# Eleven kept chunks instead of twelve, and whole V chunks beside the serial chain, in a two-layer cached-attention decode kernel

## The chip, the core and the metric

The kernel runs on one core of a Trainium2 chip. The metric is the device time of one execution in microseconds (us), and the runs' median stands for the kernel. The profile is one further execution, taken by the hardware profiler; its span (first to last instruction of the program) is a little shorter than its device time.

Engines are called as in the profile: PE is the matmul engine (PEld its weight loads), DVE the vector engine, ACT the scalar engine, POOL GpSimd, SP the queue that issues the loads.

## What is computed

One new token for each of 8 sequences goes through attention (A), an MLP mixer (B), A again and B again, with the same weights and the same K and V caches in both rounds:

```python
x = x + _A_ref(_layernorm(x, axis=-1), A_k_cache, A_v_cache, A_wq, A_wo)
x = x + _B_ref(_layernorm(x, axis=-1), B_w1, B_w2, B_w3, B_w4)
x = x + _A_ref(_layernorm(x, axis=-1), A_k_cache, A_v_cache, A_wq, A_wo)
x = x + _B_ref(_layernorm(x, axis=-1), B_w1, B_w2, B_w3, B_w4)
```

Attention has 16 query heads on 8 KV heads, 4096 cached positions, head width 256, model width 448. In B the shifted branch vanishes (the sequence length is 1), so that what is left is x + h2 with the gelu MLP of width 1792. The K and V caches together are 8 x 8 x 4096 x 256 x 2 tensors of bf16, 268 MB, and each of the two rounds needs all of them.

## The kernel before

**Chunks and places.** The caches come in chunks of 1 MB (128 partitions of 4096 bf16 elements). A unit is one (round, sequence b, KV head pair gp), with four K chunks and four V chunks. On chip there are `NC = 15` places of one chunk each (the tile `places`). A list `places` of free ones is filled in the program's order: a chunk's place goes back on it when its item has been recorded, and `emit_loads` then hands it to the next load. All cache loads are issued by SP in this one order; a load waits on SP until the instructions that still read its place are done.

**Kept chunks.** Round 2 of a sequence needs the same K and V as round 1. For two head pairs (gp 3 and gp 2) a list `kept` names chunks which stay in their places between round 1 and round 2 of the sequence: 8 K chunks (already transposed) and 4 V chunks. One more V chunk (`inner`) waits in PSUM (`away`, `back`; lines 791 to 803) and a quarter of another (`part`). So, when all 12 kept chunks of a sequence are on chip, 15 - 12 = 3 places are left for the stream of other chunks.

**Work on a chunk.** A K chunk is transposed in place by DVE (`transpose_k`, line 759, three instructions), two transposed chunks are scored by 32 matmuls of 256 columns (`scores`, line 774; 64 of 128 columns where the two places are not neighbours), then ACT takes exponentials (line 783). A V chunk takes 16 matmuls (`pv`, line 827) into a PSUM bank `o`.

**The chain.** When round 1 of sequence b is done, a serial chain of small steps makes the queries of its round 2: `half` (normalise the attention output, lines 451 to 479), `add_cols` with wo (line 365), `norm` (lines 226 to 306, with a power on POOL at line 254), the MLP (lines 383 and 365), `norm` again, and `project_q` (line 316, four blocks of 32 matmuls). It is a Python generator; each `yield` ends a step, and `step(idx)` records the next step of the generators of the kinds "chain", "last" and "rest". The kept K chunks can be scored for round 2 only when the chain has ended.

**What stands beside the chain.** `first_kept` puts off the V chunks of up to four units of other sequences (16 chunks; for the last two chains only two units, 8 chunks). `AFTER = 8` of them are placed right after round 1 of the sequence, beside the chain, and the rest between the kept K chunks of round 2. The first `AFTER + 3` of them are in the set `narrow`: each of these is loaded by two DMAs of half a chunk (line 749), and around its `pv` four steps are recorded: one before, two after its first 8 matmuls, one after it. So a half chunk of V has two steps behind it:

```python
            step(idx)
            ...
                pv(
                    st["o", g8],
                    ...
                    (lambda: (step(idx), step(idx))) if it in narrow else None,
                )
        ...
        emit_loads()
        step(idx)
```

Generators of kind "last" (they close round 2 of an earlier sequence) are stepped in the same calls. If the first kept K is reached and the chain has not ended, `while (1, b) not in state: step(...)` records the rest of it with nothing between.

The order of work in one sequence's period, in the middle of the run, is thus: round 1 of gp 2 and gp 3 (their chunks stay), interleaved with K of two other units; 8 V chunks beside the chain; 8 kept K with 8 V between them; kept V; then gp 0 and gp 1 of round 2 and the next sequence. There are eight such periods, one for each sequence.

Of the kernel before, what the change touches and what calls it, by code (L numbers as in the profile page):

```python
# [17 lines left out]
def kernel(  # L18
# [37 lines left out]
    GP = G // 2  # L56
# [5 lines left out]
    NP = 4  # L62

    kept = [(gp, 0, n) for gp in (GP - 1, GP - 2) for n in range(4)]
    kept += [(GP - 1, 1, n) for n in range(1, 4)] + [(GP - 2, 1, 2)]
    inner = (GP - 2, 1, 1)
    part = (GP - 1, 1, 0)
    Q4 = 4 * Dh
# [141 lines left out]
    def norm(x, nb, twice):  # L210

        def room(name, shape, at):
            n = shape[0] * shape[1]
            if nb < Bn:
                t = chn.tile([128, n * MID], FP32, tag=name)
                ap = t[:, 0 : n * nb]
            else:
                ap = scratch(at, n * nb)  # L220
            return ap.rearrange("p (s f b) -> p s f b", s=shape[0], f=shape[1])

        def bc(ap):
            return ap.unsqueeze(1).to_broadcast([128, 4, nb])

        xx = room("xx", (2, 4), 0)
        nc.vector.tensor_mul(xx[:, 0], x, wv[:].unsqueeze(2).to_broadcast([128, 4, nb]))
        nc.vector.tensor_mul(xx[:, 1], xx[:, 0], x)
        xs = room("xs", (1, 2), 512)[:, 0]
        nc.vector.tensor_reduce(  # L230
            xs, xx.rearrange("p s f b -> p s b f"), mybir.AxisListType.X, ALU.add
        )
        yield
        st = room_ps("st", nb).rearrange("p (s b) -> p s b", b=nb)
        nc.tensor.matmul(st, ones, xs, start=True, stop=True)  # L235
        yield
        mv = room("mv", (1, 2), 528)[:, 0]
        nc.vector.tensor_copy(mv, st)
        var = room("var", (1, 1), 608)[:, 0, 0]
        if nb == 1:  # L240
            nc.vector.scalar_tensor_tensor(
                var, mv[:, 0], mv[:, 0], mv[:, 1], ALU.mult, ALU.subtract, reverse1=True
            )
        else:
            nc.vector.tensor_mul(var, mv[:, 0], mv[:, 0])
            nc.vector.tensor_sub(var, mv[:, 1], var)


        ve = room("ve", (1, 2), 544)[:, 0]
        n = 2 if twice else 1  # L250
        rs = room("rs", (1, 2), 560)[:, 0]

        def power(k0, k1):
            nc.gpsimd.tensor_tensor(  # L254
                rs[:, k0:k1].rearrange("p n b -> p (n b)"),
                ve[:, k0:k1].rearrange("p n b -> p (n b)"),
                nhalf[:].to_broadcast([128, (k1 - k0) * nb]),
                ALU.pow,
            )

        if twice and nb == 1:
            nc.vector.scalar_tensor_tensor(
                ve[:, :, 0], var.to_broadcast([128, 2]), 0.0, eps2[:], ALU.max, ALU.add
            )
            power(0, 2)
        else:
            if twice:
                nc.vector.tensor_scalar(
                    ve[:, 1], var, 0.0, EPS * EPS / (1 + EPS), ALU.max, ALU.add
                )  # L270
                power(1, 2)
            nc.vector.tensor_scalar(ve[:, 0], var, 0.0, EPS, ALU.max, ALU.add)
            power(0, 1)
        xc = room("xc", (1, 4), 576)[:, 0]
        nc.vector.tensor_tensor(xc, x, bc(mv[:, 0]), ALU.subtract)  # L275
        yield
        if nb > 1:
            yield
        c = (1 + EPS) ** -0.5 if twice else 1.0
        rl = rs[:, n - 1]  # L280
        parts = ((0, 128, 0, 0, 3, 0), (0, 64, 64, 3, 4, 4), (64, 128, 64, 3, 4, 3))
        if nb == 1:
            nc.vector.scalar_tensor_tensor(  # L283
                xbs(1)[:, 0:4, 0], xc[:, :, 0], rl, low[:, int(twice)], ALU.mult, ALU.mult
            )
            parts = parts[1:2]
        for p0, p1, x0, f0, f1, to in parts:
            pp = slice(x0, x0 + p1 - p0)
            dst = xbs(nb)[p0:p1, to : to + f1 - f0, :]
            if nb == 1:  # L290
                nc.vector.tensor_scalar(dst, xc[pp, f0:f1], rl[pp], c, ALU.mult, ALU.mult)
            else:
                nc.vector.scalar_tensor_tensor(
                    dst,
                    xc[pp, f0:f1],
                    c,
                    rl[pp].unsqueeze(1).to_broadcast([p1 - p0, f1 - f0, nb]),
                    ALU.mult,
                    ALU.mult,
                )  # L300
        if twice and nb == 1:
            nc.vector.scalar_tensor_tensor(x, xc, rs[:, 0], x, ALU.mult, ALU.add)
        elif twice:
            nc.vector.tensor_tensor(xc, xc, bc(rs[:, 0]), ALU.mult)
            nc.vector.tensor_add(x, x, xc)
        yield
# [174 lines left out]
    locked = []  # L481
# [68 lines left out]

    tasks, items, due = [], [], []
    number, narrow = {}, set()
    AFTER = 8

    def block(k, v=None):

# [15 lines left out]
    def first_kept(b, units, before):  # L572

        k2, k3 = ((0, b, gp) for gp in keep)
        todo = list(units)
        block(todo.pop(0), before)
        if len(todo) > 2:
            block(todo.pop(0))
        block(k2)
        block(todo.pop(0), k2) if todo else block(None, k2)  # L580
        block(k3)
        block(todo.pop(0), k3) if todo else block(None, k3)
        assert not todo
        items.extend(due)
        due.clear()
        for u in units:
            due.extend((number[u], 1, c) for c in range(4))
        narrow.update(due[: AFTER + 3])
        items.extend(due[:AFTER])
        del due[:AFTER]  # L590

# [3 lines left out]
    for b in range(Bn):  # L595
# [5 lines left out]
        else:  # L601
            block((1, b, free[0]), k2)
            block((1, b, free[1]), (1, b, free[0]))
            block(None, (1, b, free[1]))
    saved = {u for units in ahead for u in units}

    def stays(it):
        n, kv, c = it
# [10 lines left out]
    loads = [it for it in items if not (tasks[it[0]][0] == 1 and (stays(it) or inside(it)))]  # L619
# [86 lines left out]
    def emit_loads(most=None):  # L706
        n = 0
        while loads and places and n != most:
            it = loads[0]
# [31 lines left out]
                src = rows.rearrange("(a p y) d -> a p (y d)", a=4, y=16)[c]  # L741
            else:
                src = rows.rearrange("(p x y) d -> x p (y d)", x=4, y=16)[c]
            if loads and it not in narrow:
                z0 = Q4 if tasks[t][0] == 1 and halfway(it) else 0
                nc.sync.dma_start(dst[:, z0:], src[:, z0:])  # L746
            else:
                for y in range(2):
                    nc.sync.dma_start(
                        dst[:, 8 * Dh * y : 8 * Dh * (y + 1)], src[:, 8 * Dh * y : 8 * Dh * (y + 1)]  # L750
                    )
# [30 lines left out]
    def exps(p_sb, zall, gp, u):  # L782
        nc.scalar.activation(  # L783
            p_sb[:, :, :, 2 * u : 2 * u + 2].rearrange("p t i x -> p x t i"),
            sc[:, 256 * u : 256 * u + 256].rearrange("p (x t i) -> p x t i", x=2, t=4),
            ACT.Exp,
            scale=scale_exp,
            accum_out=zall[:, u, gp : gp + 1],
        )
# [87 lines left out]
    gens, pairs_done, p_of = [], {}, {}  # L877

    def add_gen(kind, g, at=0, until=0, total=0):
        gens.append({"kind": kind, "g": g, "at": at, "until": until, "n": 0, "of": total})  # L880

    def step(idx):

        for kind in ("chain", "last", "rest"):
            e = next((e for e in gens if e["kind"] == kind), None)
            if e is None:
                continue
            if not e["of"] or e["n"] < e["of"] * (idx - e["at"] + 1) / max(e["until"] - e["at"], 1):
                e["n"] += 1
                if next(e["g"], gens) is gens:  # L890
                    gens.remove(e)

    def give_q(who):
# [29 lines left out]
    for idx, it in enumerate(items):  # L923
# [7 lines left out]
        n, kv, c = it  # L931
# [4 lines left out]
        kept_now = ps == 1 and (stays(it) or inside(it))  # L936
# [4 lines left out]
        if kv == 0:  # L941
# [15 lines left out]
                    oc = store[3][:, 0 : 2 * Hq].rearrange("p (j h) -> p j h", j=2)  # L957
            if not kept_now:
                transpose_k(slot)
            step(idx)  # L960
            x = c - c % 2
            scored = not paired(n, c) or c % 2 == int(late(it))
            turn = turn_p if scored and p_of and n not in p_of else None
# [13 lines left out]
                p_of[n] = p_n  # L977
            if c % 2 == 1:
                exps(p_of[n], st["z"], gp, c // 2)
            if (ps, gp, c) == (1, keep[-1], 1):  # L980
                where[(b, inner[0]), inner[1:]] = kept_place
                back(slots[kept_place])
        else:
            st = state[ps, b]
            if n in p_of:
                turn_p()
            spread_p(it)
# [1 line left out]
                spread_p(v_next[it])  # L989
            if final and gp in free and c == 1:  # L990
                rz_gp = run(z_cols(st["z"], [gp]))
            step(idx)
            if final and gp in free:
                pv_cols(oc, slot, c, gp, psv[slot_of[n]])
                if c % 2 == 1:
# [14 lines left out]
            else:  # L1010
# [6 lines left out]
                if c == 0 and pairs_done.get((ps, b), 0) % 2 == 1:  # L1017
# [5 lines left out]
                    if ps == 0:  # L1023
                        g = (first_half if done == 2 else chain)(b, st, ready)
# [8 lines left out]
                    c,  # L1033
                    gp,
                    ring_of[it],
                    (lambda: (step(idx), step(idx))) if it in narrow else None,
                )
                if ps == 0 and inside(it):
                    away(slot)
# [15 lines left out]
                slots[where[soon]][:, 0:Q4].bitcast(U32), store[4][:].bitcast(U32)  # L1055
            )
        emit_loads()
        step(idx)
    while gens:
        step(10 * len(items))  # L1060

# [63 lines left out]
```

## Time and profile before

| | |
|---|---|
| three runs | 1125.53, 1123.61, 1128.49 us; median 1125.53 |
| profiled execution | 1128.03 us, span 1126.2 us |
| mean granted PE clock | 0.634 |
| busy share of the span | PE 58%, PEld 37%, DVE 54%, ACT 15%, POOL 1% |
| DMA | 438.23 MB moved, mean 389 GB/s |
| cache loads | 125 V of 1024 KB, 166 V of 512 KB, 8 V of 768 KB, 61 K of 2048 KB, 70 K of 1024 KB |

A busy share is the time of an engine's instructions over the span; for a kernel whose loads set the pace the row of GB/s by time is the one to read, since a stretch below the steady rate is time in which the queue had nothing to move, or too little. In the table of windows each line gives a stretch, the busy time and the count of instructions of each engine, the granted clock, the DMA engines' busy share and the rate. "Idle before" in a timeline line is the engine's wait just ahead of it, with the instruction that ended the wait.

### The profile page before, as it was taken

The numbers are of one execution on the slowest core, as the hardware profiler recorded it, in microseconds if no ns is written. First come the engines' busy times: TensorE is split into PE (matmuls) and PEld (weight loads), VectorE is DVE, ScalarE is ACT, GpSimd is POOL, SyncE is SP. The second block draws the span as 40 slices with busy tenths as digits, with TensorE's granted clock in tenths as the row PEclk, the third lists the DMA queues.
The fourth block names the chain that finished last, engine by engine and source line by source line (L and its number), as shares of the span: only waits on it lengthen the run. The fifth ranks groups of instructions, "written<-read, shape, count | busy, mean of one in ns | idle before, by whom it ended". The sixth has DMA issues, their size and how long they took to land.

```text
span 1126.2 us, 30082 instructions
## 1 busy us (share of the span) xinstructions
PE 650.9 (58%) x13460; PEld 418.5 (37%) x13460; DVE 607.6 (54%) x1242; ACT 163.6 (15%) x610; POOL 16.3 (1%) x27
## 2 busy tenths in 40 slices
PE   3244477544776447554575446754477546866875
PEld 2122245322453225332353223532244324543554
DVE  4348732587316872278533784258732673576362
ACT  0011111111021111111111111111111111111020
POOL 0000000000000000000000000000000000000000
PEclk9999755766556555765656655565556655565565
DMA  9999998999999999999999999999999999899894
GB/s 360 396 425 427 423 363 331 421 425 419 344 366 425 422 412 337 402 424 423 404 325 424 425 425 389 333 426 423 422 355 352 422 422 377 333 425 416 302 420 202
DMA packets 67185, 438.23 MB, mean 389 GB/s; under 512 B 7144, under 2 KB 11120, under 8 KB 33904
## 3 DMA queue, kind: packets, MB, share of 16 engines
q1 hardware_dynamic: 66864, 435.94, 96.1%
q8 instruction: 105, 1.72, 0.6%
q10 hardware_dynamic: 192, 0.38, 0.1%
q14 instruction: 24, 0.20, 0.0%
HBM read 436.28 MB, written 0.01 MB: 387 GB/s over the span
## 4 chain that ended last, share of the span: by engine, by line
DMA 63%; PE 20%; DVE 9%; SPq 3%; issue 2%; POOL 1%; ACT 1%; DVEq 0%; ACTq 0%
DMA places<-in_A_v_cache_dram 40%; DMA places<-in_A_k_cache_dram 22%; PE o L827 6%; PE sc L774 5%; DVE places L759 4%; PE misc L316 3%; PE misc L365 3%; SPq L174 2%; DVE store L794 2%; PE misc L383 1%; POOL t L254 1%; SPq L746 1%; PE misc L235 1%; PE misc L473 1%; DMA wq_sb<-in_A_wq_dram 1%
## 5 line engine op out<-in xcount | busy, mean ns | idle before, releaser
L759 DVE STREAM_TRANSPOSE places<-places 128x512 uint32<-128x512 uint32 (+1 forms) x576 | 460.4, 857 | 131.2 <-DMA places<-in_A_k_cache_dram 123.6
L774 PE MATMUL sc<-places,qbd 128*8 128x256 bf16 (+1 forms) x5088 | 249.7, 349 | 220.0 <-DVE places L759 207.5
L827 PE MATMUL o<-places,ptw 128*8 128x256 bf16 x3968 | 242.8, 381 | 151.2 <-DMA places<-in_A_v_cache_dram 129.0
L774 PEld LDWEIGHTS <-qbd 128*8 128x8 bf16 x5088 | 132.4, 105 | 292.3 <-issue 120.6
L827 PEld LDWEIGHTS <-ptw 128*8 128x8 bf16 x3968 | 104.6, 102 | 215.7 <-issue 137.9
L783 ACT ACTIVATE p_n<-sc 128x256 bf16<-128x256 f32 x128 | 95.1, 743 | 338.2 <-PE sc L774 338.2
L919 ACT COPY ptw<-psv 128x32 bf16<-128x32 bf16 x248 | 51.8, 224 | 209.8 <-PE o L827 175.4
L468 DVE MEMSET o<- 128x256 f32 x31 | 8.4, 272 | 102.2 <-ACT ptw L919 75.6
L817 ACT CAST psv<-misc 128x128 bf16<-128x128 f32 x64 | 17.0, 265 | 308.0 <-PE misc L810 308.0
L440 DVE RECIPROCAL rz<-misc 128x8 f32<-128x8 f32 (+1 forms) x33 | 6.6, 199 | 90.3 <-PE misc L437 67.6
L365 PEld LDWEIGHTS <-wo_sb 128*128 128x128 bf16 x1280 | 39.2, 104 | 35.0 <-issue 34.9
L316 PEld LDWEIGHTS <-wq_sb 128*128 128x128 bf16 x1152 | 34.7, 104 | 32.1 <-issue 21.7
L365 PE MATMUL misc<-OT,wo_sb 128*128 128x1 bf16 x1024 | 32.0, 165 | 21.2 <-DVE OT L477 21.2
L316 PE MATMUL misc<-xb,wq_sb 128*128 128x1 bf16 x1024 | 33.2, 165 | 11.5 <-DVE xb L283 8.9
L473 PE MATMUL misc<-R,o_sb 128*128 128x8 f32 x124 | 28.2, 338 | 19.7 <-ACT o_sb L467 11.9
L473 PEld LDWEIGHTS misc<-R,o_sb 128*128 128x128 f32 x124 | 25.5, 286 | 31.4 <-ACT o_sb L467 22.9
L783 ACT ACTIVATION_READ_ACCUMULATOR p_n<-sc 128x1 f32 x128 | 33.7, 263 | 0.0
L254 POOL TENSOR_TENSOR t<-t,nhalf 128x2 f32<-128x2 f32 (+2 forms) x20 | 14.0, 703 | 1097.7 <-DVE t L275 1097.7
L339 DVE CAST qbd<-misc 32x64 bf16<-32x64 f32 x92 | 19.8, 215 | 15.2 <-PE misc L335 14.3
L383 PE MATMUL misc<-xb,w_sb 128*128 128x1 bf16 (+1 forms) x560 | 18.8, 166 | 11.8 <-DVE xb L283 9.4
L383 PEld LDWEIGHTS <-w_sb 128*128 128x128 bf16 x560 | 17.9, 105 | 19.4 <-issue 18.6
L801 DVE STREAM_TRANSPOSE places<-store 128x512 uint32<-128x512 uint32 x32 | 20.1, 685 | 4.4 <-PE sc L774 4.4
(104 smaller groups left out, 286.7 us busy)
## 6 DMA issues: line engine op xcount, KB each, us to landing
places<-in_A_v_cache_dram SPq DMA_DIRECT2D x125, 1024.0 KB, 18.0
places<-in_A_k_cache_dram SPq DMA_DIRECT2D x61, 2048.0 KB, 22.2
places<-in_A_v_cache_dram SPq DMA_DIRECT2D x166, 512.0 KB, 6.8
places<-in_A_k_cache_dram SPq DMA_DIRECT2D x70, 1024.0 KB, 16.6
places<-in_A_v_cache_dram SPq DMA_DIRECT2D x8, 768.0 KB, 4.5
wo_sb<-in_A_wo_dram SPq DMA_DIRECT2D x1, 3584.0 KB
wq_sb<-in_A_wq_dram SPq DMA_DIRECT2D x3, 1024.0 KB, 11.2
w_sb<-in_B_w_dram SPq DMA_DIRECT2D x1, 1568.0 KB
```

The source lines that it names most:

```text
L174: nc.sync.dma_start(t[:, fc * cols : (fc + 1) * cols], src[fc * 128 : fc * 128 + 128, :])
L254: nc.gpsimd.tensor_tensor(rs[:, k0:k1].rearrange("p n b -> p (n b)"), ve[:, k0:k1].rearrange("p n b -> p (n b)"), nhalf[:].to_broadcast([1 ...
L316: nc.tensor.matmul(q_ps[:, j * Hq + h, :], w, xbs(nb)[:, xi, :], start=(fc == 0), stop=(fc == 3),)
L365: nc.tensor.matmul(y_ps[:, fc, :], w[:, i, at : at + 128], rhs(i), start=start, stop=stop, skip_group_check=open is not None,)
L383: nc.tensor.matmul(h_ps[:, c * nb : c * nb + nb], w, xbs(nb)[:, xi, :], start=(fc == 0), stop=(fc == 3),)
L473: nc.tensor.matmul(ot_ps[:, j], o_sb[:].rearrange("p (i j) -> p j i", j=2)[:, j], R[:], start=True, stop=True)
L759: nc.vector.transpose(w, w)
L774: nc.tensor.matmul(sc[32 * k : 32 * k + 8, 128 * x : 128 * (x + nx)], qbd[:, ep, gp].rearrange("p a h -> p (a h)"), v, start=(n == 0), sto ...
L783: nc.scalar.activation(p_sb[:, :, :, 2 * u : 2 * u + 2].rearrange("p t i x -> p x t i"), sc[:, 256 * u : 256 * u + 256].rearrange("p (x t ...
L794: nc.vector.transpose(store[n][:].bitcast(U32), slot[:].bitcast(U32)[:, 512 * n : 512 * n + 512])
L827: nc.tensor.matmul(o_ps[32 * q : 32 * q + 8, :], ptz[:, at : at + 8], v[:, y * Dh : (y + 1) * Dh], start=False, stop=(y >= 12), skip_group ...
L919: nc.scalar.copy(ptw[:, ring_of[it], :, 6:8], psv[slot_of[it[0]]][:, it[2]])
```

## The change

- `kept` loses the V chunk (gp 2, c 2). It is loaded twice, in round 1 and in round 2. With 11 kept chunks there are 4 places for the stream.
- `AFTER` is 12: twelve put-off V chunks stand beside the chain, four between the kept K. In the last two chains all 8 stand beside it. `narrow` is these V chunks alone.
- V chunks in `narrow` are loaded whole. (Only the very last load of the program is still cut in two.)
- In `narrow` the step ahead of `pv` goes, and one step instead of two follows the first 8 matmuls; with the one after the chunk, each half chunk has one step behind it.
- A step that ends with `yield 2` (in `norm`, after the power has been given to POOL) makes the next such call pass over the chain once.
- While the chain runs (`alone`), generators of kind "last" are not stepped unless they hold the lock of `half`; `alone` is cleared at the first exponentials of the kept K.

The diff, without the lines that only rename:

```diff
     kept = [(gp, 0, n) for gp in (GP - 1, GP - 2) for n in range(4)]
-    kept += [(GP - 1, 1, n) for n in range(1, 4)] + [(GP - 2, 1, 2)]
+    kept += [(GP - 1, 1, n) for n in range(1, 4)]
...
         nc.vector.tensor_tensor(xc, x, bc(mv[:, 0]), ALU.subtract)
-        yield
+        yield 2
...
-    AFTER = 8
+    AFTER = 12
...
-        narrow.update(due[: AFTER + 3])
+        narrow.update(due[:AFTER])
...
+    calm = True
...
-            if loads and it not in narrow:
+            if loads:
                 z0 = Q4 if tasks[t][0] == 1 and halfway(it) else 0
                 nc.sync.dma_start(dst[:, z0:], src[:, z0:])
             else:
...
-        gens.append({"kind": kind, "g": g, "at": at, "until": until, "n": 0, "of": total})
-
-    def step(idx):
+        gens.append({"kind": kind, "g": g, "at": at, "until": until, "n": 0, "of": total, "skip": 0})
+
+    alone = []
+
+    def step(idx, calm=False):
 
         for kind in ("chain", "last", "rest"):
             e = next((e for e in gens if e["kind"] == kind), None)
-            if e is None:
+            if e is None or (kind == "last" and alone and not e.get("locks") and idx < len(items)):
+                continue
+            if calm and e["skip"]:
+                e["skip"] -= 1
                 continue
             if not e["of"] or e["n"] < e["of"] * (idx - e["at"] + 1) / max(e["until"] - e["at"], 1):
                 e["n"] += 1
-                if next(e["g"], gens) is gens:
+                had = len(locked)
+                got = next(e["g"], gens)
+                if len(locked) != had:
+                    e["locks"] = len(locked) > had
+                e["skip"] = 1 if got == 2 else 0
+                if got is gens:
                     gens.remove(e)
...
-            step(idx)
+            if not alone:
+                step(idx)
             x = c - c % 2
...
                 exps(p_of[n], st["z"], gp, c // 2)
+                if kept_now:
+                    alone.clear()
...
             st = state[ps, b]
+            if it in narrow and it[2] == 0 and not alone and any(e["kind"] == "chain" for e in gens):
+                alone.append(n)
             if n in p_of:
                 turn_p()
...
-            step(idx)
+            if it not in narrow:
+                step(idx)
             if final and gp in free:
...
-                    (lambda: (step(idx), step(idx))) if it in narrow else None,
+                    (lambda: step(idx, calm)) if it in narrow else None,
                 )
...
         emit_loads()
-        step(idx)
+        step(idx, it in narrow and calm)
```

## The prediction

> **What bounds the kernel now.** I read the page's rates by time and its chain of waits first, to see which resource sets the pace; then the table of windows, to price the stretches that are not at the steady rate; then PE's timeline in one of those, to see what holds it; then SP's own waits.
>
> ```profile
> GB/s 360 396 425 427 423 363 331 421 425 419 344 366 425 422 412 337 402 424 423 404 325 424 425 425 389 333 426 423 422 355 352 422 422 377 333 425 416 302 420 202
> ...
> DMA 63%; PE 20%; DVE 9%; SPq 3%; issue 2%; POOL 1%; ACT 1%; DVEq 0%; ACTq 0%
> ```
>
> The rate is flat at 421 to 427 GB/s and falls eight times: DMA is the bound, except in eight dips. One dip is one chain:
>
> ```profile
> 150.00:190.00 40.00, 31.36 (x702) 21.38 (x694) 9.74 (x45) 6.06 (x24) 1.26 (x2) 0.56 0.91 318
> 190.00:280.00 90.00, 43.02 (x896) 25.92 (x895) 59.68 (x93) 13.26 (x49) 0.00 (x0) 0.66 1.01 423
> 280.00:325.00 45.00, 33.21 (x688) 22.87 (x689) 14.76 (x52) 6.14 (x27) 1.25 (x2) 0.54 0.94 335
> 325.00:415.00 90.00, 46.46 (x900) 27.93 (x896) 58.90 (x91) 14.07 (x50) 0.00 (x0) 0.59 1.01 424
> 415.00:460.00 45.00, 33.40 (x714) 22.23 (x713) 15.51 (x55) 7.39 (x30) 1.25 (x2) 0.59 0.93 348
> ...
> 555.00:590.00 35.00, 27.24 (x574) 18.65 (x567) 10.60 (x46) 4.87 (x20) 1.26 (x2) 0.57 0.92 333
> ...
> 690.00:725.00 35.00, 27.08 (x550) 18.18 (x550) 9.73 (x44) 4.86 (x20) 1.25 (x2) 0.50 0.93 331
> ...
> 815.00:860.00 45.00, 33.48 (x676) 22.07 (x677) 17.87 (x58) 6.21 (x26) 1.25 (x2) 0.52 0.92 335
> ...
> 945.00:975.00 30.00, 24.69 (x546) 18.03 (x547) 10.08 (x43) 2.54 (x10) 1.25 (x2) 0.50 0.84 299
> ...
> 1040.00:1070.00 30.00, 24.62 (x546) 17.94 (x547) 9.49 (x43) 2.53 (x10) 1.24 (x2) 0.50 0.86 308
> ```
>
> The last column is the rate, the last but three POOL (two powers, the mark of a chain). Time lost in a stretch is its length times (1 - rate/424): 10.0, 9.5, 8.1, 7.5, 7.7 and 9.5 us in the first six dips (52.2), 8.8 and 8.2 in the last two (17.1), 69.2 in all. Check: 438.23 MB at 424 GB/s take 1033.5; with 69.2, 6.0 at the start (0 to 45 at 367), 14.5 at the end (1110 on, at 44) and 3 us of small change that is 1126, the span. So the sum below may be made in bytes and lost time.
>
> What holds a dip, on PE:
>
> ```profile
> 292.29 0.60 PE L827 MATMUL o<-places,ptw 128*8 128x256 bf16 x8
> 292.82 1.01 PE L365 MATMUL misc<-OT,wo_sb 128*128 128x1 bf16 x32
> 293.76 0.60 PE L827 MATMUL o<-places,ptw 128*8 128x256 bf16 x8
> ...
> 296.69 0.60 PE L827 MATMUL o<-places,ptw 128*8 128x256 bf16 x8
> 298.54 1.05 PE L383 MATMUL misc<-xb,w_sb 128*128 128x1 bf16 x28 [1.25 <-DVE xb L283]
> 299.52 0.60 PE L827 MATMUL o<-places,ptw 128*8 128x256 bf16 x8
> 300.05 0.91 PE L383 MATMUL misc<-xb,w_sb 128*128 128x1 bf16 x28
> 300.88 0.60 PE L827 MATMUL o<-places,ptw 128*8 128x256 bf16 x8
> ...
> 305.70 0.60 PE L827 MATMUL o<-places,ptw 128*8 128x256 bf16 x8
> 307.41 1.16 PE L316 MATMUL misc<-xb,wq_sb 128*128 128x1 bf16 x32 [1.12 <-DVE xb L283]
> ```
>
> From start to start, half a V chunk takes 0.53 us of PE, a block of 32 chain matmuls 0.94, one of 28 0.83. PE stands before the blocks that need the norm (1.25 and 1.12 us), with landed V behind them in its queue. SP waits for PE:
>
> ```profile
> SPq L749 <- PE o L827: 137.0, 101, 2.8
> ```
>
> The half loads wait for places that V on PE has not freed, not for memory. In this dip the 8 V chunks and the chain take 292.3 to 317.0 (first kept scores), 24.7 us; 8 chunks of 1.049 MB at 424 are 19.8, and the three places drain.
>
> **Part 1, one chunk less kept.** Eight more loads of 1.049 MB, one for each sequence, 8.39 MB. They fall in gp 2 of round 2, beside K that DMA limits (325 to 415: 424 GB/s, DVE 58.9 of 90 us), so nothing hides them: 8.39/0.424 = +19.8 us. At the mean of the page (389) 21.6; less than 19.8 is excluded by the flat top. The Trainium skill ("HBM Reference", section "Specifications (TRN2)") speaks against the change: it gives about 358 GB/s as a core's share. By that ceiling, as an estimate, the dips at 299 to 348 would hold only 26 us and the added bytes would cost 23, so that no gain would be left; the same page has about 425 for a core that streams alone, and the windows at 423 and 424 decide for that.
>
> **Part 2, the chain beside 12 V (six chains).** From the chain's start PE has, in the built order of the changed kernel: 24 halves x 0.53 = 12.7; blocks 6 x 0.94 + 4 x 0.83 = 9.0; the fp32 block after the copy of o (291.33 to 292.29) 1.0 and its wait 0.5; two norm sums x 0.54 (296.15 to 296.69) 1.1. Together 24.2 us for 12 V, against 12 x 2.47 = 29.6 us that DMA needs. The waits go: between the norm's sum and the block that needs it there are now four halves (2.1 us) where the way over DVE and POOL takes 1.9 (296.69 to 298.54), and before the tanh result three halves (1.6) for 1.2. So DMA sets the pace again, with 5.4 us to spare, if the places turn round in time. A place's round: landing, use, release. V's use is at most 2 x (0.53 + 0.94) = 2.94, in the mean 2.0. Landing of a whole chunk near an empty queue is not in these dips; nearest are the five 1 MB and smaller loads issued by line 746 between 1040 and 1070, 4.5 to 8.5 us, median 6.8. Four places allow 4 x 2.47 = 9.9 us; 6.8 + 2.0 = 8.8 fits, 8.5 + 2.94 = 11.4 does not and would make V's pace 2.86, a loss of 12 x 0.39 = 4.7 us a chain. I take the median row and leave 1.5 us a chain for the ends of the dip; bounds 0 and 4.7. Less than 0 is excluded, as 424 is the top. Sum: 52.2 - 9.0 = -43.2 us.
>
> At the chain's end three things are later than before: one q block (0.94), cast and spread without V between (1.6, 313.2 to 314.8), the first kept scores (2.2, 317.02 to 319.2): 4.7 us until the kept places begin to come free. About 3.2 chunks are then under way, 7.9 us, which hide it; without that cover it would be the 1.5 a chain above, three times over.
>
> **Part 3, the last two chains** have 8 V as before, but now with 16 steps beside them instead of all. After the last V remain: norm (304.26 to 307.41) 3.1, less a half 0.5; four q blocks 3.8; cast and spread 1.6; scores 2.2: 10.2 us until a place comes free, plus some 1.2 before its load moves. Cover: 3.2 chunks less the quarter of the 768 KB load, 7.3. Loss at least 4.1; at most today's 8.5. I take 5.5, as the V themselves run at DMA's pace: 17.1 - 11.0 = -6.1 us.
>
> **The rest, at nothing.** Whole loads instead of halves: PE's first half now waits for the whole chunk, and a load on SP waits for the second half of V (1.47 us later than the first); behind it on SP stand only the next loads, and both are in the round above. SP issues 74 fewer V loads, 0.33 us each. "last" is held back until the first kept exponentials: its fp32 block (0.96) and copy then stand between kept scores, 1.5 us a sequence, where 7 kept places come free in a row; 12 us in all if that cover were gone. Five more K pairs come as one load; three more are scored by 32 wide matmuls, 1.88 us like 64 narrow ones. The pass-over after POOL moves no instruction to another queue.
>
> Sum: 1128.0 (profiled execution, 1.8 above its span) + 19.8 - 43.2 - 6.1 = 1098.5. The profiled execution is 2.5 above the median, so the forecast is 1096.
>
> **Rivals.** A, nothing is left in six dips and 4.1 in the two: 1128.0 + 19.8 - 52.2 - 8.9 = 1086.7, 1084 on the runs' scale. For it: 5.4 us to spare. Against it: the dips begin up to 10 us before the chain's V (282 to 290), where K pairs hold places.
> B, the round is long (11.4): 4.7 in each of six, 6.5 in two: 1128.0 + 19.8 - 24.0 - 4.1 = 1119.7, 1117. For it: the half loads at 290 to 314 took 4.1 to 7.4 us to land, at a queue not full.
> C, slower: whole chunks make the place's round the bound. The change loses once six dips keep 32.4 us (52.2 - 19.8), 5.4 each, V's pace 2.92, a round of 11.7 us. At 13 us the pace is 3.25, 9.4 a chain, and with no gain in the last two the time is 1128.0 + 19.8 + 4.2 = 1152, 1149 on the runs' scale. For it: longest landing and longest use give 11.4 already. Against it: they do not meet in every chunk.
> D, the fourth place is taken up elsewhere (pairs of K, the chunk's own second load) and dips stay: 1145. The built order shows 12 whole V in a row and one step a half, so little speaks for it.
>
> **Chances.** Forecast (1088 to 1107) 0.47, A 0.17, B 0.19, C 0.14, D 0.03. A measurement can tell about 0.5%, 5.6 us. Faster: 0.47 + 0.17 + 0.19 = 0.83; 0.03 of C lies about its turning point: same 0.03; slower 0.14. The range 1081 to 1121 leaves out the lowest part of A and what lies above B.
>
> **What would show it.** Right: 446.6 MB moved; the six dips at 400 GB/s or more, the last two at 340 to 380; PE in a dip waiting for V's landing and no longer for the norm. Wrong: dips of 300 to 350 with SP waiting for PE at line 828 (C), or a dip moved to the kept K after the chain.

## The result, and the profile after

The changed kernel takes 1122.65 us (median of 20 runs, 1120.6 to 1124.61) against 1126.36 for the kernel before (20 runs): a ratio of 0.9963, 95% interval 0.9953 to 0.9972. It is faster, by 3.7 us, where 30 were forecast; 1122.65 lies above the range (1081 to 1121). The profiled execution took 1120.6 us with a span of 1118.8, 7.4 less than before. It is the lowest of the 20, 2.0 below their median, and the profiled execution of the kernel before is 1.7 above its own, so the accounts below, made on these two, are some 4 us too kind.

The page of the changed kernel, rates by time and the chain of waits:

```profile
GB/s 360 396 424 428 421 416 383 420 427 421 409 359 425 423 423 411 365 427 427 418 409 373 427 425 417 357 419 423 423 420 356 425 422 418 306 429 416 313 406 199
...
DMA 52%; PE 23%; DVE 18%; SPq 3%; issue 2%; ACT 1%; POOL 0%; DVEq 0%; ACTq 0%
```

The eight dips are there still, but narrow: most fill one slice of 28 us. The windows (length, five engines, clock, DMA share, rate) say the same:

```profile
207.00:285.00 78.00, 39.41 (x780) 22.36 (x777) 62.97 (x96) 13.20 (x48) 0.00 (x0) 0.59 1.01 424
285.00:335.00 50.00, 36.48 (x743) 23.81 (x740) 10.88 (x49) 6.51 (x26) 1.25 (x2) 0.53 0.94 380
...
840.00:865.00 25.00, 18.43 (x338) 11.49 (x337) 6.40 (x27) 3.40 (x13) 0.55 (x1) 0.50 0.88 350
...
950.00:975.00 25.00, 18.38 (x419) 13.38 (x420) 11.93 (x35) 4.18 (x14) 0.55 (x1) 0.52 0.75 294
...
1040.00:1070.00 30.00, 20.92 (x444) 14.39 (x447) 12.32 (x37) 3.70 (x14) 0.55 (x1) 0.50 0.78 306
```

By the same formula as in the prediction (of the windows some are left out here) the six dips now lose 3.4, 5.2, 4.5, 4.2, 5.0 and 4.4 us (26.7), the last two 7.7 and 8.3 (16.0): 42.7 against 69.2 before. 446.59 MB were moved against 438.23, 19.7 us more at 424. 69.2 - 42.7 - 19.7 = 6.8 of the 7.4 us that the span lost. Of the signs that the prediction gave for being right, the bytes came true, but not the rates: the six dips stand at 350 to 396 GB/s in these windows instead of 400 or more, the last two at 294 and 306 instead of 340 to 380.

In the chain itself V's pace is DMA's, 411 GB/s from 290 to 317, and PE waits for V to land, no longer for the norm:

```profile
312.19 0.60 PE L828 MATMUL o<-places,ptw 128*8 128x256 bf16 x8 [1.46 <-DMA places<-in_A_v_cache_dram]
312.73 1.01 PE L316 MATMUL misc<-xb,wq_sb 128*128 128x1 bf16 x32
```

Where the rest of a dip lies is seen in one timeline of the second dip (start, length, instruction; the SP line stands for two issues, the first at 317.26, the second ending at 325.56):

```profile
316.61 0.60 PE L828 MATMUL o<-places,ptw 128*8 128x256 bf16 x8
...
317.26 8.30 SPq L747 DMA_DIRECT2D places<-in_A_v_cache_dram  x2
...
321.08 1.02 PE L775 MATMUL sc<-places,qbd 128*8 128x256 bf16 x16
...
322.25 1.02 PE L775 MATMUL sc<-places,qbd 128*8 128x256 bf16 x16
...
323.21 1.01 PE L473 MATMUL misc<-R,o_sb 128*128 128x8 f32 x4
...
324.16 1.02 PE L828 MATMUL o<-places,ptw 128*8 128x256 bf16 x16
```

At 316.61 the 12th V has its last matmuls and its place is loaded again at 317.26. Then come the last q block, the cast, the kept scores (321.08 to 323.2), the fp32 block of "last", and only at 324.16 the next V, whose place goes out at 325.23. For 8.0 us SP issues nothing. By the trace's packet records 2.06 MB were still to move at 318.0 and nothing was at 325.0.

The six dips all have this pause, from the load into the 12th V's place to the next one. It is 6.2 us in the first, 8.0 in the second and 7.1 in the other four; the first, second and sixth as windows:

```profile
185.06:191.23 6.17, 4.85 (x90) 2.88 (x89) 1.75 (x9) 0.60 (x3) 0.00 (x0) 0.50 0.87 361
317.26:325.23 7.97, 5.93 (x94) 3.88 (x93) 2.96 (x13) 1.52 (x6) 0.00 (x0) 0.50 0.71 293
...
851.06:858.18 7.12, 5.79 (x94) 3.80 (x93) 2.96 (x13) 1.52 (x6) 0.00 (x0) 0.50 0.73 283
```

Length times rate is what still moved in a pause: 2.0 to 2.3 MB, which fill 4.7 to 5.5 us at 424. By the formula above the six pauses lose 0.9, 2.5, 1.9, 1.9, 1.9 and 2.4 us, 11.4 together. The 3.5 us behind each pause run at 230 to 238 GB/s and lose 1.6 more, 9.4 in the six, as the queue has to fill again. The remaining 5.9 us of the 26.7 are spread over the rest of the dips. A pause by itself costs nothing: from 368.46 to 382.51 SP issues nothing for 14.0 us, and the rate is 422, because 5.9 MB were queued.

Of SP's waits for the matmuls of V the longest, 7.6 us, is the gap in the second dip:

```profile
SPq L747 <- PE o L828: 252.8, 146, 7.6
```

### The profile page after: what moved, and what is told of

Same layout as the page of the kernel before. It is cut to its first block, busy times and chain, and to the rows that moved or that the text cites. A ratio compares the mean times of both kernels' runs of the same rounds, so it can differ in the third digit from the quotient of the medians.

```text
span 1118.8 us, 29781 instructions
## 1 busy us (share of the span) xinstructions
PE 650.1 (58%) x13364; PEld 409.6 (37%) x13364; DVE 603.8 (54%) x1242; ACT 162.7 (15%) x610; POOL 16.4 (1%) x27
## 2 busy tenths in 40 slices
DMA packets 55808, 446.59 MB, mean 399 GB/s; under 512 B 5881, under 2 KB 9857, under 8 KB 11649
## 4 chain that ended last, share of the span: by engine, by line
DMA 52%; PE 23%; DVE 18%; SPq 3%; issue 2%; ACT 1%; POOL 0%; DVEq 0%; ACTq 0%
DMA places<-in_A_v_cache_dram 27%; DMA places<-in_A_k_cache_dram 23%; DVE places L760 12%; PE sc L775 9%; PE o L828 7%; PE misc L316 3%; PE misc L365 3%; SPq L174 2%; DVE qbd L339 1%; DVE store L795 1%; DVE places L802 1%; SPq L747 1%; PE misc L473 1%; ACT p_n L784 1%; DMA wq_sb<-in_A_wq_dram 1%
## 5 line engine op out<-in xcount | busy, mean ns | idle before, releaser
L775 PEld LDWEIGHTS <-qbd 128*8 128x8 bf16 x4992 | 129.1, 104 | 306.5 <-DVE places L760 158.5
L339 DVE CAST qbd<-misc 32x64 bf16<-32x64 f32 x92 | 19.8, 215 | 18.3 <-PE misc L335 17.3
L437 PE MATMUL misc<-zm,one 128*128 128x8 f32 (+1 forms) x66 | 17.7, 341 | 17.3 <-DVE zm L429 9.9
L437 PEld LDWEIGHTS misc<-zm,one 128*128 128x128 f32 x66 | 14.8, 277 | 27.0 <-DVE zm L429 12.4
## 6 DMA issues: line engine op xcount, KB each, us to landing
w_sb<-in_B_w_dram SPq DMA_DIRECT2D x3, 448.0 KB, 11.5
```

The source lines that it names most:

```text
L339: nc.vector.tensor_copy(qbd[32 * a : 32 * a + 32, :, :, a, :], qs.rearrange("p e (f g u h) -> p (e f) u g h", f=2, u=2, h=2)[:, :, u],)
L437: nc.tensor.matmul(z_ps, ones, zm[:], start=True, stop=True)
L775: nc.tensor.matmul(sc[32 * k : 32 * k + 8, 128 * x : 128 * (x + nx)], qbd[:, ep, gp].rearrange("p a h -> p (a h)"), v, start=(n == 0), sto ...
```

## The experiments

Ratios are to the kernel before, with 95% intervals. The first four ran together, so did the next four and the last four.

**Twelve chunks kept, new order** (three stream places, the bytes of before).

```diff
-    kept += [(GP - 1, 1, n) for n in range(1, 4)]
+    kept += [(GP - 1, 1, n) for n in range(1, 4)] + [(GP - 2, 1, 2)]
```

> The new order with the 12th chunk kept: 8.39 MB less to load, three places for the stream. Theory (the new order lets DMA set the pace beside the chain; what is lost is the 8 us after the chain in which no place comes free, covered only by what is queued): -19.8 us for the bytes, but the queue that covers the end of each chain is one chunk (2.47 us) shorter, +19.8 over eight chains, and V's pace is limited by three places, 0 to 3 us a chain more: 1120 to 1146. Rival (the fourth place is worth nothing, the order does it all): 1103.

1151.26 us, 1.0223 (1.0176 to 1.027), slower than the upper end expected. The rival is ruled out: in the new order with whole loads the place that the dropped chunk left is worth more than its bytes cost. With whole chunks three places do not even keep V's pace: beside the chain the rate is 375 GB/s (293 to 322) where four places gave 411.

**Fourteen places in all, eleven kept.**

```diff
-    NC = 15
+    NC = 14
```

> The changed kernel with 14 places in all and 11 kept: its bytes, its order, but three places for the stream. Beside the run with 12 kept it differs by the 8.39 MB and by the place that the 12th chunk has. Theory: one chunk less under way at the end of each chain, +2.5 us each, and V's pace limited by three places: 1140 to 1165. Rival (the fourth place is worth nothing): 1123, and 20 us above the run with 12 kept by the bytes alone.

1168.78 us, 1.0387 (1.0351 to 1.0422). It has the order and the three stream places of the run before and 8.39 MB more: +17.5 us between the medians, with ranges of 1143.63 to 1155.27 and 1165.13 to 1172.43. That is the price of the bytes, which the prediction put at 19.8. Against the changed kernel the one place less costs 46 us, more than the 42 at the theory's upper end. In its second dip the rate is 404 GB/s ahead of the chain (275 to 297), 360 beside it (297 to 330) and 295 behind it (330 to 345).

**Fourteen V beside the chain.**

```diff
-    AFTER = 12
+    AFTER = 14
```

> The changed kernel with 14 V beside the chain instead of 12 and two instead of four between the kept K (six chains; the last two have only 8 V and stay as they are). Theory: the chain ends beside the 13th V, the 14th follows at once, and the stretch without a freed place falls from 8 to about 4 us, less than the 5.2 us that are queued: 3 to 4 us a chain back in six, 1100 to 1107. Rival (the 8 us stretch only moves to the kept K, which then have two V fewer between them): 1120 to 1127.

1107.84 us, 0.9841 (0.9815 to 0.9868), 14.8 below the changed kernel. The same stretch in its timeline (with the 13th and 14th V at 317.32 and 318.48, the kept scores at 320.34):

```profile
315.69 3.04 SPq L747 DMA_DIRECT2D places<-in_A_v_cache_dram  x2
...
317.32 1.03 PE L828 MATMUL o<-places,ptw 128*8 128x256 bf16 x16 [0.60 <-ACT ptw L930]
...
318.48 1.02 PE L828 MATMUL o<-places,ptw 128*8 128x256 bf16 x16
...
319.54 3.91 SPq L747 DMA_DIRECT2D places<-in_A_k_cache_dram  x2
320.34 1.88 PE L775 MATMUL sc<-places,qbd 128*8 128x256 bf16 x32
```

Issues now follow at 315.69, 318.40, 319.54 and 323.12: the longest pause is 3.6 us instead of 8.0, inside what is queued. All that was changed is that two V went from between the kept K to ahead of them, so that the last steps of the chain have V beside them too. In windows of 50 us around the six dips (60 for the fifth) this run loses 10.8 us and the changed kernel 27.5. So the stretch at the chain's end is shown to be what most of the six chains' loss came from.

**The old order with eleven kept chunks** (the kernel before, one chunk less kept, nothing else).

```diff
-    kept += [(GP - 1, 1, n) for n in range(1, 4)] + [(GP - 2, 1, 2)]
+    kept += [(GP - 1, 1, n) for n in range(1, 4)]
```

> The kernel before with 11 kept chunks and nothing else changed: four places, 8 V beside the chain, four steps around each, half loads. Theory: +19.8 us for the bytes, at most one chunk more under way in each chain, -2.5 us each, -20 in all, if PE's pace stays what it is: 1126 to 1140. Rival (the fourth place is what lifts the dips, not the order): 1115 to 1123.

1125.25 us, 0.9985 (0.9967 to 1.0004), just under the expected range and no different from before. Two of its eight dips:

```profile
150.00:195.00 45.00, 35.01 (x772) 23.80 (x761) 10.11 (x47) 7.39 (x29) 1.26 (x2) 0.55 0.94 349
300.00:325.00 25.00, 20.41 (x444) 14.32 (x444) 6.66 (x27) 4.44 (x17) 0.55 (x1) 0.60 0.96 358
```

With the others at 351, 343, 324, 346, 318 and 329 GB/s (25, 25, 30, 30, 30 and 25 us long) its dips lose 46.7 us, 22.5 less than before: the fourth place alone just pays for its bytes. So of the changed kernel's 26.5 us less in the dips, 22.5 are the place's and only some 4 the order's. Between the medians, which are free of the luck of single executions, the order is worth 2.6 us (1125.25 against 1122.65), and the intervals just overlap.

**Two steps a half in the last two chains**, on top of 14 V.

```diff
...
+        if len(units) == 2:
+            few.update(due[:AFTER])
...
-            if it not in narrow:
+            if it not in narrow or it in few:
                 step(idx)
...
-                    (lambda: step(idx, calm)) if it in narrow else None,
+                    (lambda: (step(idx), step(idx)) if it in few else step(idx, calm)) if it in narrow else None,
...
-        step(idx, it in narrow and calm)
+        step(idx, it in narrow and it not in few and calm)
```

> The run with 14 V beside the chain, and in the last two chains, which have 8 V alone, two steps of the chain behind each half chunk as before the change. Theory (with one step a half, ten steps of these chains are left when the V are used up, and no place comes free meanwhile): the loss of the last two falls from about 8 us each to 5 to 7: 1102 to 1106. Rival (the steps only move into V's pace, and the loss is the same 8): 1107 to 1111.

1102.19 us, 0.9782 (0.9766 to 0.9798), in the expected range and the lowest median of all. The window of the seventh chain, first with one step a half (the run with 14 V), then with two:

```profile
920.00:960.00 40.00, 29.79 (x639) 20.88 (x639) 14.28 (x48) 4.99 (x19) 1.25 (x2) 0.50 0.83 330
```

```profile
920.00:960.00 40.00, 32.02 (x733) 23.04 (x733) 17.10 (x54) 5.70 (x22) 1.25 (x2) 0.57 0.94 372
```

In the changed kernel itself SP stands still at this place for 11.3 us:

```profile
953.02 0.33 SPq L747 DMA_DIRECT2D places<-in_A_v_cache_dram  x1
...
964.28 0.33 SPq L747 DMA_DIRECT2D places<-in_A_k_cache_dram  x1
```

**Twelve kept, new order, halves.**

```diff
-            if loads:
+            if loads and it not in narrow:
                 z0 = Q4 if tasks[t][0] == 1 and halfway(it) else 0
```

(and the `kept` line of the first run)

> The run with 12 kept chunks and the new order, with V beside the chain loaded in halves as before the change. Theory 1 (a place that holds a whole chunk comes round too slowly for three places: landing and use take more than 7.4 us): halves give the 20 to 30 us back, 1115 to 1128. Theory 2 (three places are too few whatever is loaded, because the queue at the chain's end is a chunk shorter): 1140 to 1152.

1127.42 us, 1.0003 (0.9991 to 1.0015), in the range of theory 1. Half loads give 23.8 us back where there are three places. The windows beside the chain, of 12 kept with whole chunks, of this run, and of the changed kernel:

```profile
293.00:322.00 29.00, 19.60 (x392) 12.13 (x384) 4.48 (x26) 2.30 (x11) 1.25 (x2) 0.50 0.98 375
```

```profile
290.00:319.00 29.00, 21.06 (x445) 12.53 (x443) 4.30 (x25) 2.08 (x10) 1.25 (x2) 0.50 1.02 404
```

```profile
290.00:317.00 27.00, 20.54 (x452) 12.92 (x444) 4.30 (x25) 2.08 (x10) 1.25 (x2) 0.50 1.01 411
```

It also says that the new order by itself, with the places, bytes and load sizes of before, wins nothing (+0.8 us): what it takes out of the chain comes back behind it, where SP pauses for 8.1 us at the second chain. This order includes the hold of "last", which is priced in the next run for the changed kernel alone; the order without it was not run with twelve kept.

**"last" not held back**, on the changed kernel.

```diff
-            if e is None or (kind == "last" and alone and not e.get("locks") and idx < len(items)):
+            if e is None:
```

> The changed kernel with generators of kind last stepped beside the chain again. Theory (the stretch without a freed place comes from the kept scores standing ahead of the first V after the chain; the held-back block of last adds 1 us to it, its sum 2 us to the next): -3 to -8 us, 1114 to 1120. Rival (the hold protects V's pace in the chain): 1123 to 1130.

1114.29 us, 0.9887 (0.9872 to 0.9903): 8.4 us below the changed kernel. The first V after the chain now stands right behind the kept scores; the fp32 block and the sums of "last" are gone from between:

```profile
317.43 5.87 SPq L747 DMA_DIRECT2D places<-in_A_v_cache_dram  x2
...
321.86 1.06 PE L828 MATMUL o<-places,ptw 128*8 128x256 bf16 x16
```

The pause of SP is 5.5 us instead of 8.0, and V's pace in the chain does not suffer (408 GB/s from 290 to 318). The hold of the change was a loss.

**Halves with four places**, on the changed kernel (the `if loads and it not in narrow` line alone).

> The changed kernel with V beside the chain loaded in halves. With four places V's pace is DMA's in either form, so that halves change only the rate of the packets (394 to 418 instead of 410 to 424 GB/s in the dips) and issue time: +1 to +6 us, 1123 to 1129. If whole chunks still cost by their round, halves are faster: 1112 to 1120.

1118.35 us, 0.9925 (0.9908 to 0.9941): 4.3 below the changed kernel, inside the second expectation. Whole chunks were no gain there. The cause stays open. V's pace in the second chain is the same (411 GB/s from 291 to 318), and the pause there is as long and as well covered (8.05 us at 296 GB/s, against 7.97 at 293). The two profiled executions took 1119.92 and 1120.6 us, so that their traces can hardly show where 4.3 us between medians lie.

**Thirteen V, and sixteen.**

```diff
-    AFTER = 12
+    AFTER = 13
```

> The changed kernel with 13 V beside the chain: its last two steps stand beside the 13th, and the kept scores come right after it, with the fp32 block of last and then the 14th V behind. If the stretch without a freed place is what the change loses, the time falls by steps with it: about 4.5 us without a freed place, 1107 to 1114, between the runs with 12 and with 14. If 14 was faster for another reason (fewer V between kept K), the time is half way at most by chance; no fall at all, 1120 to 1124, would speak for that.

1111.58 us, 0.9867 (0.9827 to 0.9907): between 12 and 14, in the expected range. At the second chain the pause is 4.5 us (321.45 to 325.91). So pauses of 8.0, 5.5, 4.5 and 3.6 us there (12 V, 12 V without the hold, 13 V, 14 V) go with 1122.65, 1114.29, 1111.58 and 1107.84 us.

```diff
-    AFTER = 12
+    AFTER = 16
```

> All 16 V beside and right behind the chain, none between the kept K. Theory: the chain ends at the 13th as with 14, so nothing more is won there, and the kept K, whose first pair gives one place back and not two, then stand alone: +1 to +2 us a chain in six against the run with 14, 1112 to 1120. Rival (the more V in a row the better): 1100 to 1107.

1115.14 us, 0.9898 (0.9854 to 0.9941): slower than 14 by 7, in the expected range. But its profile has no dip at the second chain (408 GB/s from 285 to 340) and deep ones at the third and sixth (149 from 465 to 470, 74 from 860 to 865), where SP pauses for some 10 us each until scores of kept K free a place. Why it does so at these two and not at the second is not shown, nor then "the first pair gives one place back" as the reason.

**The best so far without the hold, and with halves.** On the run with two steps a half, first the line of "last" as above:

> 14 V beside the chain, two steps a half in the last two chains, and generators of kind last no longer held back. Where the stretch after the chain is short already, the held blocks meet queued loads: 0 to -4 us against the run with the first two, 1098 to 1102. If their cost is the same wherever they stand, -8: 1094.

1103.6 us, 0.9799 (0.9751 to 0.9848): no different from 1102.19, and above both expectations. Once V stand before the kept scores, the hold costs nothing that can be measured.

Then with halves as well:

> The same with V beside the chain in halves. If halves won 4 us in the changed kernel by shortening the stretch after the chain (a half is free before the last block), little is left to win: -1 to +3, 1098 to 1103. If they won it by V's pace beside the chain, -4: 1094 to 1097.

1107.55 us, 0.9829 (0.9789 to 0.9869), 4 above the run before it in the median and above both expectations, with ranges that overlap (1102.76 to 1106.54, 1105.85 to 1108.76). Halves win nothing once the pause is gone; whether they lose is not settled.

## Why the prediction was wrong, step by step

- **What bounds the kernel** held: bytes at 424 GB/s and eight dips. The account closes again after the change, to 0.6 us.
- **Part 1** (+19.8 us for the bytes) held: 8.36 MB more were moved, and the two runs that differ by them alone differ by 17.5 us.
- **Part 2, beside the chain**, held: 12 V run at DMA's pace there (411 GB/s), and PE waits for landing and no longer for the norm (the waits of the q blocks fell from 11.5 to 3.6 us over the run, those that were for the norm from 8.9 to next to nothing). The row taken for a chunk's landing was 6.8 us; it was 7.8 to 8.8, median 8.1, with some 2 MB queued. With the prediction's 2.0 for V's use that is a round of 10.1 us, just over the 9.9 that four places allow, and the pace held all the same; with three places, which allow 7.4, it did not (375 GB/s). What Part 2 did not separate is the place from the order: by the old order with eleven kept, most of the gain in the dips comes with the fourth place even at PE's old pace.
- **The step that failed is the end of the chain in Part 2**: "4.7 us until the kept places begin to come free. About 3.2 chunks are then under way, 7.9 us, which hide it". Neither figure is what matters there. Loads go out in one order, and the next one had the place of the V behind the kept scores, so the scores' own end freed nothing: by the program, of the first pair one place goes to the chunk that comes back from PSUM, and the other is handed on only behind that V. The way to the end of the scores did take about 4.7 us, but the V adds 1.0, and "last", costed at nothing because kept places "come free in a row", put its sum and its fp32 block into the pause, 1.5 more. That makes the 7.1 us of four dips; in the first dip the fp32 block stands behind the V (6.2), in the second PE also stood still for 0.7 us (8.0). The cover was 4.7 to 5.5 us, not 7.9: a place whose bytes have moved, but which has not been used yet, I had counted as queued, and only bytes that are still to move cover a pause. So the pauses lose 11.4 us where nothing was allowed, and the rest of the six dips 15.3 where 9.0 were, 9.4 of it while the empty queue fills again: 26.7 us stayed, +17.7.
- **Part 3** was too small in the same way: 16.0 instead of 11.0, +5.0. The 10.2 us until a place is free were 11.3; the cover was again too long (207 and 200 GB/s over the two pauses, 2.3 MB or 5.5 us, where 7.3 were assumed).
- The two terms make 22.7 us; 1098.5 + 22.7 = 1121.2, against 1120.6 of the profiled execution. On the runs' scale it is 1096 + 22.7 = 1118.7 against 1122.65; the 4 us between are those by which the two profiled executions are too kind.
- **The rivals.** B was nearest in size but for a reason that did not act. C named whole chunks and the round of places; with four places it did not act, with three it does (375 against 404 GB/s). The last line of the prediction named the thing that happened, "a dip moved to the kept K after the chain", and gave it neither a price nor a chance.
- The whole change is then three things: a place (-22.5 us in the dips, by the old order with eleven kept), its bytes (+17.5 to +20), and an order that, with its whole loads, is worth some 2.6 us with four places and, with halves, nothing with three. In that order the hold of "last" cost 8.4 us and whole loads 4.3, and two more V ahead of the kept scores are worth 14.8, each taken alone. These do not add up: with 14 V the hold costs nothing.

## What to carry to other kernels

When a queue of loads is fed by freed buffers, list the issues in their one order and ask of each which instruction frees its buffer; a pause between two of them that outlasts the bytes really still to move is a loss, however well the average pace fits. Here pauses of 7 us behind 2 MB cost time, and one of 14 us with 6 MB queued did not. Work that is taken off a serial stretch tends to land right behind it, where the buffers are just as few, so price the first few microseconds after the stretch as carefully as the stretch. A buffer's round, from issue over landing to the end of use, is worth comparing with the time of N transfers for N buffers: here four held the pace with 10.1 us against 9.9, three did not. With three, loading and freeing halves of a buffer brought the rate from 375 to 404 GB/s.

## What the runs showed of the hardware that I had not expected

In the changed kernel nine 1 MB loads, issued from 290 to 314 behind some 2 MB of others, took 7.8 to 8.8 us from issue to landing.

The burst of loads in the second dip does not end at full rate, and the next one does not begin at it. From 318 to 322 the rate is 416 GB/s, in the next three microseconds 238, 90 and 8, from 325 to 326 nothing moves, and from 326 to 327 it is 203. The load that SP issued at 325.23, with the queue empty, moved nothing before 326.

With three places whole chunks were 23.8 us slower than halves, with four 4.3 us (for a reason that is open), and with the pause removed not slower at all.
